# A cosine-attention and MLP-mixer kernel: token MLP per head pair, transposes by DMA, loads and norm work moved

## The chip, the cores and the metric

The kernel runs on one core of a Trainium2 chip. The metric is the device time of one execution in microseconds (us); lower is better. Every ratio is to runs of the kernel before on the same chip in the same rounds. A profiled span runs from the first to the last instruction of the core; a timed run is about 2 us longer than its own span. The profile of the kernel before is of an execution of 465.7 us, below the median of 467.4.

Engines in the profile: PE is TensorE (matmuls), PEld its weight loads, DVE is VectorE, ACT is ScalarE, POOL is GpSimd, SP is SyncE, which only issues DMAs. "L214" is a line of the kernel that was profiled.

## The reference

Eight batches, twelve heads, 448 tokens, head size 64. In float32:

```
q_n = q / (norm(q) + 1e-6);  k_n = k / (norm(k) + 1e-6)        # over the head dimension
attn = softmax(q_n @ k_n^T / tau)                              # tau = 0.1
x    = attn @ v                                                # to (8, 448, 768)
u    = x + (relu(x^T @ w_tok1) @ w_tok2)^T                     # token MLP, 448 -> 256 -> 448
out  = u + relu(u @ w_ch1) @ w_ch2                             # channel MLP, 768 -> 1536 -> 768
```

## The kernel before

The kernel works on 48 head pairs: 8 batches with 6 pairs each. One pass of its main loop, a *slot*, scores one pair and does the value matmuls of the pair before it. The mixer (both MLPs) waits in a queue, and a slot takes pieces from it to fill TensorE. The engines run in order, each through its own list of instructions, so the order in the text is the order on each engine.

The norms of a pair go through three engines: squares on POOL, the sum and the reciprocal on DVE, the root as a logarithm and an exponential on ACT. Then POOL scales.

```python
def squares(i, act_q=False):          # POOL (the first q on ACT)
    ...nc.gpsimd.tensor_mul(out=sq[:, a], in0=src, in1=src)
def sums(i):                          # DVE
    nc.vector.tensor_reduce(out=...["ssq"][...], in_=pipe[i]["sq"][:], axis=AXX.X, op=ALU.add)
def rnorms(n, p0=0, p1=HP):
    nc.scalar.activation(out=rn, in_=ssq, func=AF.Ln, bias=tiny[:])
    nc.scalar.activation(out=rn, in_=rn, func=AF.Exp, scale=0.5)
    nc.vector.tensor_scalar_add(out=rn, in0=rn, scalar1=EPS_NORM)      # 112 x 16 numbers, SBUF to SBUF
    nc.vector.reciprocal(out=rn, in_=rn)
def tpose(i):                         # 8 transposes on TensorE, one DVE copy
    ...
    for a, src in enumerate((st["kn"], st["qn"])):
        for c in range(NCH):
            nc.tensor.transpose(pst[:, a, c, :], src[:, c], id16[:SC, :SC])
    nc.vector.tensor_copy(out=qk[:], in_=pst[...])
```

The token MLP runs per batch, after the sixth pair. Its last step adds x to the product in PSUM with four identity matmuls that write runs of neighbouring columns:

```python
def m_tok1(b, tt, dh):                # 16 matmuls of 384 columns per batch
    ...
def m_tok2(b, dt):
    for tt in range(TT):
        nc.tensor.matmul(psU[:], rt16[b][:, tt, dt * 128:(dt + 1) * 128], w2t[...], ...)
    for m in range(4):
        nc.tensor.matmul(psU[:, lo:lo + (128 if m < 3 else 64)], x16[b][:, m, ...], rhs, ...)
    nc.vector.tensor_copy(out=ut[:, dt, span(b)], in_=psU[:])
```

## Time and profile before

| | before |
|---|---|
| median of timed runs | 467.4 us (466.4 to 468.4) |
| profiled span | 463.9 us |
| PE busy | 415.4 us (90%) |
| last matmul ends near | 459 us |

The page of the kernel before shows the span in 40 slices of 11.6 us. A digit is the busy share of a slice in tenths; PEclk is the clock granted to TensorE.

```profile
PE   0505889999999999999999999999999999999995
PEclk9999999999999999999999999999999999999998
```

TensorE is full from the seventh slice to the end, and starved before. The waits view of PE names what ended its idle time (columns: waiting instruction and its line, the instruction it waited for, us in total, times, longest). First, the stretch from 0 to 70 us:

```profile
PE psS_1_290 L199 <- ACT pt_251 L201: 11.0, 1, 11.0
PE pst_145 L183 <- DVE kn_143 L175: 9.1, 1, 9.1
PE psS_0_400 L199 <- DVE qk_365 L185: 3.8, 1, 3.8
```

From 70 us on, PE waited six times for an exponential, each time 1.1 us, and that is nearly all:

```profile
PE psS_0_1336 L199 <- ACT pt_1236 L201: 1.1, 1, 1.1
```

The timeline (start us, busy us, engine, line, what) shows the price of each kind of work in the full stretch. The distance between starts counts here, not the busy time, as matmuls overlap.

```profile
231.66 0.54 PE L246 MATMUL psU_4_3258<-w2t,rt_3_2919 128*128 128x448 f16 x2
232.04 0.36 PE L252 MATMUL psU_4_3258<-id_86,x_3_2062 128*128 128x128 f16 x4
232.24 0.36 PE L183 MATMUL pst_3266<-id_86,kn_3056 112*128 112x112 f16 x4
232.44 0.36 PE L183 MATMUL pst_3266<-id_86,qn_3054 112*128 112x112 f16 x4
```

Four transposes take 0.20 us (232.24 to 232.44), and the four identity matmuls of the token MLP take 0.20 us too (232.04 to 232.24).

### The profile page before, as it was taken

What the parts mean: (1) busy time and instruction counts of PE and PEld (TensorE: products, weight loads), DVE (VectorE), ACT (ScalarE), POOL (GpSimd) and SP (SyncE); (2) the same over time, 40 slices, a digit from 0 to 9 for tenths busy, and PEclk for the clock granted to TensorE, in tenths of its full rate; (3) what the DMA queues carried; (4) which work ended last, traced back from release to release, by engine and by line L of the source; (5) the groups of instructions that cost most, each with busy time, mean ns of one, the idle gap of its engine ahead of it and who ended that gap; (6) DMA issues with size and microseconds to landing.
All of it is one profiled execution on the core that took longest, in us unless ns stands there. A gap on an engine that the chain in (4) does not pass through costs nothing.

```text
span 463.9 us, 9519 instructions
## 1 busy us (share of the span) xinstructions
PE 415.4 (90%) x4136; PEld 250.1 (54%) x4136; DVE 218.9 (47%) x442; ACT 232.1 (50%) x262; POOL 218.8 (47%) x220
## 2 busy tenths in 40 slices
PE   0505889999999999999999999999999999999995
PEld 0203556556654566555655566556655666556563
DVE  2558659555564455445645445445735343224000
ACT  2324666775467544574457443674367534520410
POOL 4699698678374834374383725474472200000000
PEclk9999999999999999999999999999999999999998
DMA  9997999951485046721574065902100001000012
GB/s 205 237 235 175 223 204 229 209 120 32 125 188 119 1 129 154 167 47 37 134 192 102 1 165 117 206 9 78 52 35 1 35 35 56 15 34 35 34 54 83
DMA packets 72842, 50.02 MB, mean 108 GB/s; under 512 B 44449, under 2 KB 68449, under 8 KB 72801
## 3 DMA queue, kind: packets, MB, share of 16 engines
q1 hardware_dynamic: 69408, 44.05, 39.6%
q0 software_dynamic: 3392, 5.37, 6.3%
q8 instruction: 32, 0.52, 0.5%
q14 instruction: 10, 0.07, 0.1%
HBM read 43.78 MB, written 11.01 MB: 118 GB/s over the span
## 4 chain that ended last, share of the span: by engine, by line
PE 84%; ACT 6%; DVE 4%; POOL 2%; issue 2%; DMA 1%; SPq 0%; ACTq 0%; POOLq 0%
DMA qh_105<-in_q_dram 1%; DVE kn_324 L175 1%; DVE ssq_118 L157 1%; ACT pt_630 L201 1%; ACT pt_482 L201 1%; ACT pt_1042 L201 1%; DVE ssq_126 L157 0%; POOL sq_207 L152 0%; PE psF_2_1_5429 L279 0%; PE psF_2_0_5377 L279 0%; PE psF_1_1_5303 L279 0%; PE psF_0_0_5164 L279 0%; PE psF_2_1_4787 L279 0%; PE psF_2_0_4717 L279 0%; PE psF_1_1_4651 L279 0%
## 5 line engine op out<-in xcount | busy, mean ns | idle before, releaser
L260 PEld LDWEIGHTS <-wc1t 128*128 128x128 f16 x576 | 51.5, 97 | 52.0 <-issue 10.7
L279 PEld LDWEIGHTS <-gt_2_3862 128*128 128x128 f16 x168 | 15.3, 98 | 12.8 <-issue 2.6
L279 PEld LDWEIGHTS <-gt_1_2351 128*128 128x128 f16 x168 | 15.4, 98 | 12.5 <-issue 2.6
L279 PEld LDWEIGHTS <-gt_0_804 128*128 128x128 f16 x168 | 15.5, 98 | 11.4 <-issue 1.5
L279 PEld LDWEIGHTS <-gt_3_5342 128*128 128x128 f16 x168 | 15.9, 98 | 9.6
L228 PEld LDWEIGHTS <-w1t 128*128 128x128 f16 x128 | 10.9, 97 | 8.0 <-issue 2.6
L199 PE MATMUL psS_1_290<-qk_185 64*128 64x448 f16 x4 | 0.9, 557 | 11.0 <-ACT pt_251 L201 11.0
L183 PE MATMUL pst_145<-id_86,kn_143 112*128 112x112 f16 x4 | 0.6, 291 | 9.1 <-DVE kn_143 L175 9.1
L199 PEld LDWEIGHTS <-qk_185 64*128 64x128 f16 x8 | 0.5, 104 | 13.6 <-issue 12.9
L285 DVE COPY ost_0_6031<-psF_0_0_6032 128x384 f32<-128x384 f32 x1 | 0.6, 557 | 15.2 <-PE psF_0_0_6032 L282 15.2
L164 ACT ACTIVATE rn_119<-ssq_118,tiny 112x16 f32<-112x16 f32 x3 | 0.9, 307 | 12.1 <-DVE ssq_118 L157 12.1
L175 POOL TENSOR_TENSOR qn_5044<-qh_4311,rn_4315 112x512 f16<-112x512 f32 x1 | 1.0, 1041 | 10.3 <-DVE rn_4315 L167 10.3
L164 ACT ACTIVATE rn_109<-ssq_108,tiny 112x16 f32<-112x16 f32 x3 | 0.9, 304 | 8.6 <-DVE ssq_108 L157 8.6
L183 PEld LDWEIGHTS <-kn_143 112*128 112x128 f16 x4 | 0.3, 129 | 9.1 <-DVE kn_143 L175 9.1
L175 DVE TENSOR_TENSOR kn_324<-kh_116,rn_119 112x512 f16<-112x512 f32 x1 | 4.7, 4745 | 0.0
L282 PEld LDWEIGHTS <-ut_0_803 128*128 128x128 f16 x42 | 3.5, 98 | 1.8
L282 PEld LDWEIGHTS <-ut_1_2350 128*128 128x128 f16 x42 | 3.5, 98 | 1.8
L282 PEld LDWEIGHTS <-ut_2_3861 128*128 128x128 f16 x42 | 3.5, 98 | 1.8
L282 PEld LDWEIGHTS <-ut_3_5341 128*128 128x128 f16 x42 | 3.5, 98 | 1.8
L175 POOL TENSOR_TENSOR qn_3954<-qh_3191,rn_3195 112x512 f16<-112x512 f32 x1 | 1.0, 1042 | 7.3 <-PE psU_3_3986 L252 7.3
L199 PE MATMUL psS_0_400<-qk_365 64*128 64x448 f16 x4 | 0.9, 564 | 3.8 <-DVE qk_365 L185 3.8
L152 POOL TENSOR_TENSOR sq_2301<-qh_2033 112x512 f32<-112x512 f32 x1 | 1.0, 1039 | 6.9 <-DVE ssq_1701 L157 6.9
(1726 smaller groups left out, 1299.7 us busy)
## 6 DMA issues: line engine op xcount, KB each, us to landing
wc1t<-in_moe_w_ch_dram POOLq DMA_DIRECT2D x2, 1152.0 KB, 13.0
wc2t<-in_moe_w_ch_dram POOLq DMA_DIRECT2D x2, 1152.0 KB, 15.4
vs_107<-in_v_dram SPq DMA_DIRECT2D x1, 672.0 KB, 7.8
qh_115<-in_q_dram SPq DMA_DIRECT2D x1, 672.0 KB, 10.2
kh_116<-in_k_dram SPq DMA_DIRECT2D x1, 672.0 KB, 12.2
vs_117<-in_v_dram SPq DMA_DIRECT2D x1, 672.0 KB, 8.3
qh_123<-in_q_dram SPq DMA_DIRECT2D x1, 672.0 KB, 10.8
kh_124<-in_k_dram SPq DMA_DIRECT2D x1, 672.0 KB, 12.6
```

Source lines behind the costliest of these rows:

```text
L152: nc.gpsimd.tensor_mul(out=sq[:, a], in0=src, in1=src)
L157: nc.vector.tensor_reduce(out=half[i // HP]["ssq"][:, :, lo:lo + 2 * NCH], in_=pipe[i]["sq"][:], axis=AXX.X, op=ALU.add)
L164: nc.scalar.activation(out=rn, in_=ssq, func=AF.Ln, bias=tiny[:])
L175: eng.tensor_tensor(out=dst[:].rearrange("p c g e -> p g c e"), in0=src, in1=_bcast_free(rn, E), op=ALU.mult)
L183: nc.tensor.transpose(pst[:, a, c, :], src[:, c], id16[:SC, :SC])
L199: nc.tensor.matmul(psS[:, hh, j, 0:S], qk[hb:hb + 64, c * SC:c * SC + 128], qk[hb:hb + 64, S:2 * S], start=True, stop=True)
L201: nc.scalar.activation(out=st["pt"][:, cg], in_=psS[0:SC, :, :, 0:S], func=AF.Exp, scale=inv_tau)
L228: nc.tensor.matmul(psR[:], w1t[:, m, tt * 128:(tt + 1) * 128], x16[b][:, m, dh * DH:(dh + 1) * DH], start=(m == 0), stop=(m == 3))
L260: nc.tensor.matmul(psG[:], wc1t[:, dt, ct * 128:(ct + 1) * 128], ut[:, dt, span(b)], start=(dt == 0), stop=(dt == DT - 1))
L279: nc.tensor.matmul(psF[:], rows(gt, ct), wc2t[:, ct, dh * DH:(dh + 1) * DH], start=(ct == 0), stop=False)
L282: nc.tensor.matmul(psF[:, 128 * i:128 * (i + 1)], rows(ut, 3 * dh + i), id16[:], start=False, stop=(i == 2))
L285: nc.vector.tensor_copy(out=o[:, 0:DH], in_=psF[:])
```

## The change

It moves work off the full TensorE and fills its empty start. Four parts:

1. The token MLP runs per head pair, one slot behind the pair's value matmuls, instead of per batch.
2. q is loaded like k, in runs of 1 KB instead of 256 B. Token 4p+c then sits in partition p, chunk c, so the tokens of x are permuted as well. w_tok1 is loaded in that order; the identity matmuls put x back in order by writing every fourth column of PSUM.
3. From pair 12 on, q and k are transposed by DMA, issued from SyncE two slots ahead.
4. The norm work of early pairs starts later, three slots ahead, and each early pair has its own norms.

```diff
-    def tpose(i): ...for every pair
+    DMA_FROM = 12
+    def dma_tpose(i):
+        for a, src in enumerate((st["kn"], st["qn"])):
+            nc.sync.dma_start_transpose(out=qk[:, a], in_=src[:].rearrange("p c g e -> p (c g e)"))
 ...
-            nc.tensor.matmul(psR[:], w1t[:, m, tt * 128:(tt + 1) * 128],
-                             x16[b][:, m, dh * DH:(dh + 1) * DH], start=(m == 0), stop=(m == 3))
+    def m_tok1(i):
+        for tt in range(TT):
+            for m in range(NCH):
+                nc.tensor.matmul(psR[:, tt, :], w1t[:, m, tt * 128:(tt + 1) * 128], st["x"][:, m, :], ...)
 ...
-        for m in range(4):
-            nc.tensor.matmul(psU[:, lo:lo + (128 if m < 3 else 64)], x16[b][...], rhs, ...)
+        for c in range(NCH):
+            nc.tensor.matmul(psU[:].rearrange("d (p c) -> d c p", c=NCH)[:, c, :], st["x"][:, c, :],
+                             id16[:, LEAD[c]:LEAD[c] + SC], start=False, stop=(c == NCH - 1))
 ...
+    load_at = at({p: p - 6 if p < 13 else max(p - 8, (p - 1) // 2) for p in range(9, NP_ALL)})
+    sq_at = at({p: p - 3 if p < 10 else max(p - 6, 2 + p // 2) for p in range(3, NP_ALL)})
+    sc_at = at({p: p - 2 if p < DMA_FROM else p - 3 for p in range(2, NP_ALL)})
+    tok_at = at({p: max(p + 2, 3 if p < 1 else 4) for p in range(NP_ALL)})
 ...
+            for p in sc_at.get(i, ()):  scaled(p, dve="k" if p < 4 else "")
+            for p in sq_at.get(i, ()):  squares(p)
+            if i in (7, 8):             weights_ch2(i - 7)
+            if (i + 2) % HP == 0 ...:   cast_v((i + 2) // HP)
             (score, value matmuls, token MLP, pieces of the channel MLP)
+            for p in sq_at.get(i, ()):
+                sums(p)
+                if p < 15:              rnorm1(p)
```

More of the change, by code (lines that the diff above doesn't have):

```diff
@@ L49 @@
     NPAIR = H // 2
+    NP_ALL = B * NPAIR
     HP = 3
-    REM = S - 3 * 128
+    NHALF = 2 * B
     inv_tau = 1.0 / float(tau)
     EPS_NORM = 1e-6
-    COLS = (0, 128, 256, S - 128)
+    COLS = (0, SC, 2 * SC, S - 128)
+    LEAD = (0, 0, 0, 128 - SC)
+    DMA_FROM = 12
     cst = ctx.enter_context(tc.tile_pool(name="cst", bufs=1))
     qkv = ctx.enter_context(tc.tile_pool(name="qkv", bufs=3))
-    nrm = ctx.enter_context(tc.tile_pool(name="nrm", bufs=2))
+    nrm = ctx.enter_context(tc.tile_pool(name="nrm", bufs=3))
     att = ctx.enter_context(tc.tile_pool(name="att", bufs=3))
     ptp = ctx.enter_context(tc.tile_pool(name="ptp", bufs=2))
-    xp = ctx.enter_context(tc.tile_pool(name="xp", bufs=2))
     mix = ctx.enter_context(tc.tile_pool(name="mix", bufs=2))
@@ L78 @@
     nc.gpsimd.memset(tiny[:], 1e-18)
-    w1t = cst.tile([128, 4, T], FP16, name="w1t")
+    w1t = cst.tile([128, NCH, T], FP16, name="w1t")
     w2t = cst.tile([128, TT, S + 384], FP16, name="w2t")
@@ L83 @@
     wc2t = cst.tile([128, CT, D], FP16, name="wc2t")
+    nc.gpsimd.memset(w1t[:], 0.0)
     NV = 3
@@ L90, with weights_ch1, weights_ch2, load_qk @@
         vts.append(vt)
-    NHALF = 2 * B
     half = {}
     pipe = {}
-    x16 = {}
     pairt = {}
     def weights_tok():
-        nc.gpsimd.memset(w1t[0:64, 3, :], 0.0)
-        nc.gpsimd.dma_start(out=w1t[:, 0:3, :],
-                            in_=moe_w_tok1[0:384].rearrange("(c p) t -> p c t", p=128))
-        nc.gpsimd.dma_start(out=w1t[64:128, 3, :], in_=moe_w_tok1[384:448])
-        w2r = moe_w_tok2.rearrange("(tt p) s -> p tt s", p=128)
-        nc.gpsimd.dma_start(out=w2t[:, :, 0:S], in_=w2r)
-        nc.gpsimd.dma_start(out=w2t[:, :, S:S + 384], in_=w2r[:, :, 0:384])
-    def weights_ch1():
-        for i in range(2):
-            nc.gpsimd.dma_start(out=wc1t[:, 3 * i:3 * i + 3, :],
-                                in_=moe_w_ch1[384 * i:384 * (i + 1)].rearrange("(t p) c -> p t c", p=128))
-    def weights_ch2():
-        for i in range(2):
-            nc.gpsimd.dma_start(out=wc2t[:, 6 * i:6 * i + 6, :],
-                                in_=moe_w_ch2[768 * i:768 * (i + 1)].rearrange("(t p) d -> p t d", p=128))
-    def load_qk(n, lo=0, hi=6):
-        b, h0 = n // 2, 6 * (n % 2)
+        w1r = moe_w_tok1.rearrange("(p c) t -> p c t", c=NCH)
+        nc.gpsimd.dma_start(out=w1t[0:SC, 0:3, :], in_=w1r[:, 0:3, :])
+        nc.gpsimd.dma_start(out=w1t[128 - SC:128, 3, :], in_=w1r[:, 3, :])
+        nc.gpsimd.dma_start(out=w2t[:, :, 0:S], in_=moe_w_tok2.rearrange("(tt p) s -> p tt s", p=128))
+    def weights_ch1(i):
+        n = C // 2
+        nc.gpsimd.dma_start(out=wc1t[:, :, n * i:n * i + n],
+                            in_=moe_w_ch1[:, n * i:n * i + n].rearrange("(t p) c -> p t c", p=128))
+    def weights_ch2(i):
+        nc.gpsimd.dma_start(out=wc2t[:, 6 * i:6 * i + 6, :],
+                            in_=moe_w_ch2[768 * i:768 * (i + 1)].rearrange("(t p) d -> p t d", p=128))
+    def load_qk(i):
+        n, j = i // HP, 2 * (i % HP)
+        b, h = n // 2, 6 * (n % 2) + j
         if n not in half:
@@ L125, in load_qk @@
                            rn=nrm.tile([SC, 2, 6 * NCH], FP32, name=f"rn_{n}", tag="rn"))
-        nc.sync.dma_start(out=half[n]["q"][:, lo:hi].rearrange("p g c e -> p (g c) e"),
-                          in_=q[b, h0 + lo:h0 + hi].rearrange("g (c p) e -> p (g c) e", p=SC))
-        nc.sync.dma_start(out=half[n]["k"][:, lo:hi].rearrange("p g c e -> p g (c e)"),
-                          in_=k[b, h0 + lo:h0 + hi].rearrange("g (p c) e -> p g (c e)", c=NCH))
+        for nm, src in (("q", q), ("k", k)):
+            nc.sync.dma_start(out=half[n][nm][:, j:j + 2].rearrange("p g c e -> p g (c e)"),
+                              in_=src[b, h:h + 2].rearrange("g (p c) e -> p g (c e)", c=NCH))
     def load_v(n):
@@ L142, in sides, with squares @@
         return hf["q"][:, j:j + 2], hf["k"][:, j:j + 2]
-    def squares(i, act_q=False):
+    def squares(i, on_act=False):
         st = pipe[i] = {}
-        sq = nrm.tile([SC, 2, 2 * NCH, E], FP32, name=f"sq_{i}", tag="sq")
+        sq = nrm.tile([SC, 2, 2 * NCH, E], FP32, name=f"sq_{i}", tag="sq", bufs=2)
         for a, src in enumerate(sides(i)):
             src = src.rearrange("p g c e -> p (g c) e")
-            if act_q and a == 0:
+            if on_act:
                 nc.scalar.activation(out=sq[:, a], in_=src, func=AF.Square)
@@ L167, in rnorms, with rnorm1, scaled @@
         nc.vector.reciprocal(out=rn, in_=rn)
-    def scaled(i, dve_k=False):
+    def rnorm1(i):
+        rnorms(i // HP, i % HP, i % HP + 1)
+    def scaled(i, dve=""):
         lo = 2 * NCH * (i % HP)
@@ L172, in scaled @@
             dst = pipe[i][nm] = att.tile([SC, NCH, 2, E], FP16, name=f"{nm}_{i}", tag=nm)
-            eng = nc.vector if dve_k and a else nc.gpsimd
+            eng = nc.vector if nm[0] in dve else nc.gpsimd
             rn = half[i // HP]["rn"][:, a, lo:lo + 2 * NCH].rearrange("p (g c) -> p g c", g=2)
@@ L176, in scaled, with qk_tile @@
                               in1=_bcast_free(rn, E), op=ALU.mult)
+    def qk_tile(i):
+        pipe[i]["qk"] = att.tile([128, 2, NCH, SC], FP16, name=f"qk_{i}", tag="qk")
+        return pipe[i]["qk"]
     def tpose(i):
@@ L183, in tpose @@
                 nc.tensor.transpose(pst[:, a, c, :], src[:, c], id16[:SC, :SC])
-        qk = att.tile([128, 2, S], FP16, name=f"qk_{i}", tag="qk")
-        nc.vector.tensor_copy(out=qk[:], in_=pst[:].rearrange("p a c s -> p a (c s)"))
-        st["qk"] = qk
+        nc.vector.tensor_copy(out=qk_tile(i)[:], in_=pst[:])
+    def dma_tpose(i):
+        st = pipe[i]
+        qk = qk_tile(i)
+        for a, src in enumerate((st["kn"], st["qn"])):
+            nc.sync.dma_start_transpose(out=qk[:, a], in_=src[:].rearrange("p c g e -> p (c g e)"))
     def score(i, cg):
         st = pipe[i]
-        qk = st["qk"][:].rearrange("p a s -> p (a s)")
+        qk = st["qk"][:].rearrange("p a c s -> p (a c s)")
         if cg == 0:
@@ L204, in pv @@
         st = pipe[i]
-        b, pj = i // NPAIR, i % NPAIR
-        if b not in x16:
-            x16[b] = xp.tile([128, 4, D], FP16, name=f"x16_{b}", tag="x16")
+        if hh == 0:
+            st["x"] = att.tile([128, NCH, 128], FP16, name=f"x_{i}", tag="x")
         vt = half[i // HP]["vt"]
         g = 2 * (i % HP) + hh
-        hid = 2 * pj + hh
         psO = ps.tile([128, 4, E + 2], FP32, name=f"psO_{i}_{hh}", tag="b")
@@ L217, in pv @@
         nc.vector.reciprocal(out=rec[:], in_=psO[:, :, E])
-        nc.vector.tensor_tensor(out=x16[b][:, :, hid * E:(hid + 1) * E], in0=psO[:, :, 0:E],
+        nc.vector.tensor_tensor(out=st["x"][:, :, hh * E:(hh + 1) * E], in0=psO[:, :, 0:E],
                                 in1=_bcast_free(rec[:], E), op=ALU.mult)
-    rt16 = {}
-    def m_tok1(b, tt, dh):
-        if b not in rt16:
-            rt16[b] = mix.tile([128, TT, D], FP16, name=f"rt16_{b}", tag="rt16", bufs=1)
-        psR = ps.tile([128, DH], FP32, name=f"psR_{b}_{tt}_{dh}", tag="b")
-        for m in range(4):
-            nc.tensor.matmul(psR[:], w1t[:, m, tt * 128:(tt + 1) * 128],
-                             x16[b][:, m, dh * DH:(dh + 1) * DH], start=(m == 0), stop=(m == 3))
-        nc.vector.tensor_scalar_max(out=rt16[b][:, tt, dh * DH:(dh + 1) * DH], in0=psR[:], scalar1=0.0)
+    def m_tok1(i):
+        st = pipe[i]
+        psR = ps.tile([128, TT, 128], FP32, name=f"psR_{i}", tag="b")
+        for tt in range(TT):
+            for m in range(NCH):
+                nc.tensor.matmul(psR[:, tt, :], w1t[:, m, tt * 128:(tt + 1) * 128], st["x"][:, m, :],
+                                 start=(m == 0), stop=(m == NCH - 1))
+        st["r"] = att.tile([128, TT, 128], FP16, name=f"r_{i}", tag="r")
+        nc.vector.tensor_scalar_max(out=st["r"][:], in0=psR[:], scalar1=0.0)
     def span(b):
@@ L237, in place, with m_tok2 @@
         return 128 * m if b % 2 == 0 else (64 + 128 * m if m < 3 else 0)
-    def m_tok2(b, dt):
+    def m_tok2(i):
+        st = pipe[i]
+        b, dt = i // NPAIR, i % NPAIR
         if b // 2 not in pairt:
@@ L243, in m_tok2 @@
         ut = pairt[b // 2][0]
-        psU = ps.tile([128, S], FP32, name=f"psU_{b}_{dt}", tag="b")
+        psU = ps.tile([128, S], FP32, name=f"psU_{i}", tag="b")
         for tt in range(TT):
-            nc.tensor.matmul(psU[:], rt16[b][:, tt, dt * 128:(dt + 1) * 128],
-                             w2t[:, tt, 0:S] if b % 2 == 0 else w2t[:, tt, 384:384 + S],
+            nc.tensor.matmul(psU[:], st["r"][:, tt, :], w2t[:, tt, 0:S],
                              start=(tt == 0), stop=False)
-        for m in range(4):
-            lo = place(b, m)
-            rhs = id16[:] if m < 3 else id16[:, 64:128]
-            nc.tensor.matmul(psU[:, lo:lo + (128 if m < 3 else 64)], x16[b][:, m, dt * 128:(dt + 1) * 128], rhs,
-                             start=False, stop=(m == 3))
-        nc.vector.tensor_copy(out=ut[:, dt, span(b)], in_=psU[:])
+        for c in range(NCH):
+            nc.tensor.matmul(psU[:].rearrange("d (p c) -> d c p", c=NCH)[:, c, :], st["x"][:, c, :],
+                             id16[:, LEAD[c]:LEAD[c] + SC], start=False, stop=(c == NCH - 1))
+        if b % 2 == 0:
+            nc.vector.tensor_copy(out=ut[:, dt, 0:S], in_=psU[:])
+        else:
+            nc.vector.tensor_copy(out=ut[:, dt, S + 64:2 * S], in_=psU[:, 0:384])
+            nc.vector.tensor_copy(out=ut[:, dt, S:S + 64], in_=psU[:, 384:S])
     def m_ch1(b, ct):
@@ L295, in ns, with ch_units @@
         return n * cols / 2.4
-    def mixer_units(b):
-        first = [(ns(DH, 4), lambda tt=tt, dh=dh: m_tok1(b, tt, dh)) for dh in range(NDH) for tt in range(TT)]
-        first += [(ns(3 * S), lambda dt=dt: m_tok2(b, dt)) for dt in range(DT)]
-        return first, [(ns(S, DT), lambda ct=ct: m_ch1(b, ct)) for ct in range(CT)]
-    def out_units(b):
-        return [(ns(DH, 13), lambda m=m, dh=dh: m_ch2(b, m, dh))
-                for m in range(3 + b % 2) for dh in range(NDH)]
-    def braid(a, c):
-        got, i, j = [], 0, 0
-        while i < len(a) or j < len(c):
-            if j >= len(c) or (i < len(a) and i * len(c) <= j * len(a)):
-                got.append(a[i]); i += 1
-            else:
-                got.append(c[j]); j += 1
-        return got
-    NP_ALL = B * NPAIR
+    def ch_units(b):
+        return ([(ns(S, DT), lambda ct=ct: m_ch1(b, ct)) for ct in range(CT)]
+                + [(ns(DH, 13), lambda m=m, dh=dh: m_ch2(b, m, dh))
+                   for m in range(3 + b % 2) for dh in range(NDH)])
     queue = []
-    fed = [0.0, 0.0]
+    fed = [0.0]
     def feed(budget, least=0.0):
@@ L328, in feed, with at @@
             done += t
-        fed[1] += done
+    def at(slots):
+        got = {}
+        for p, s in slots.items():
+            got.setdefault(s, []).append(p)
+        return got
+    load_at = at({p: p - 6 if p < 13 else max(p - 8, (p - 1) // 2) for p in range(9, NP_ALL)})
+    sq_at = at({p: p - 3 if p < 10 else max(p - 6, 2 + p // 2) for p in range(3, NP_ALL)})
+    sc_at = at({p: p - 2 if p < DMA_FROM else p - 3 for p in range(2, NP_ALL)})
+    tok_at = at({p: max(p + 2, 3 if p < 1 else 4) for p in range(NP_ALL)})
@@ L331 @@
     with tc.manual_schedule():
-        load_qk(0, 0, 2)
-        load_qk(0, 2, 6)
+        load_qk(0)
+        load_qk(1)
         load_v(0)
-        load_qk(1)
+        for p in range(2, 5):
+            load_qk(p)
         load_v(1)
-        load_qk(2)
-        squares(0, act_q=True)
+        for p in range(5, 9):
+            load_qk(p)
+        squares(0, on_act=True)
         sums(0)
-        rnorms(0, 0, 1)
-        squares(1)
-        scaled(0, dve_k=True)
+        rnorm1(0)
+        squares(1, on_act=True)
@@ L343 @@
+        squares(2)
+        scaled(0, dve="qk")
         tpose(0)
-        squares(2)
+        cast_v(0)
         sums(1)
-        rnorms(0, 1, 2)
-        cast_v(0)
-        score(0, 0)
-        scaled(1, dve_k=True)
-        tpose(1)
-        score(0, 1)
-        sums(2)
-        rnorms(0, 2, 3)
-        scaled(2, dve_k=True)
-        weights_tok()
-        squares(3)
-        sums(3)
-        rnorms(1, 0, 1)
-        for i in range(NP_ALL + 1):
-            b, pj = i // NPAIR, i % NPAIR
-            if i + 8 >= 9 and (i + 8) % HP == 0 and (i + 8) // HP < NHALF:
-                load_qk((i + 8) // HP)
-            if i % HP == 0 and i // HP + 2 < NHALF:
-                load_v(i // HP + 2)
-            if i == 0:
-                squares(4)
-                scaled(3, dve_k=True)
-            if i == 1:
-                squares(5)
-                scaled(4, dve_k=True)
-                cast_v(1)
-                weights_ch1()
-            if i == 2:
-                scaled(5, dve_k=True)
-            if i >= 4 and i + 2 < NP_ALL:
-                scaled(i + 2)
-            if 6 <= i + 6 < NP_ALL:
-                squares(i + 6)
-            if i == 6:
-                weights_ch2()
-            if (i + 3) % HP == 0 and 2 <= (i + 3) // HP < NHALF:
-                cast_v((i + 3) // HP)
-            quota = sum(t for t, _ in queue) / (NPAIR - pj + 1) if queue else 0.0
-            if i == NP_ALL:
-                pv(i - 1, 0)
-                pv(i - 1, 1)
-            else:
-                if i:
-                    score(i, 0)
-                feed(quota * 0.3)
-                if i:
-                    pv(i - 1, 0)
-                feed(quota * 0.2, 500.0)
-                if i and i + 1 < NP_ALL:
-                    tpose(i + 1)
-                if i:
-                    score(i, 1)
-                feed(quota * 0.3)
-                if i:
-                    pv(i - 1, 1)
-                feed(quota * 0.2)
-            if i < 2:
-                sums(4 + i)
-                rnorms(1, 1 + i, 2 + i)
-            if i >= 1 and i + 5 < NP_ALL:
-                sums(i + 5)
-                if (i + 5) % HP == 2:
-                    rnorms((i + 5) // HP)
-            if pj == 0 and i:
-                first, second = mixer_units(b - 1)
-                queue += braid(first, out_units(b - 2) if b >= 2 else []) + second
@@ L412 @@
-        queue += out_units(B - 1)
+        rnorm1(1)
+        scaled(1, dve="qk")
+        sums(2)
+        rnorm1(2)
+        for i in range(NP_ALL + 2):
+            for p in load_at.get(i, ()):
+                load_qk(p)
+            if (i + 4) % HP == 0 and 2 <= (i + 4) // HP < NHALF:
+                load_v((i + 4) // HP)
+            if DMA_FROM <= i + 2 < NP_ALL:
+                dma_tpose(i + 2)
+            for p in sc_at.get(i, ()):
+                scaled(p, dve="k" if p < 4 else "")
+            for p in sq_at.get(i, ()):
+                squares(p)
+            if i == 0:
+                weights_tok()
+            if i in (2, 4):
+                weights_ch1(i // 4)
+            if i in (7, 8):
+                weights_ch2(i - 7)
+            if (i + 2) % HP == 0 and 1 <= (i + 2) // HP < NHALF:
+                cast_v((i + 2) // HP)
+            left = 6 - (i - 2) % NPAIR
+            quota = max(sum(t for t, _ in queue) - 2000.0, 0.0) / left
+            if i < NP_ALL:
+                score(i, 0)
+            feed(quota * 0.25)
+            if 0 < i <= NP_ALL:
+                pv(i - 1, 0)
+            for p in tok_at.get(i, ()):
+                m_tok1(p)
+            feed(quota * 0.25, 400.0)
+            if i + 1 < min(DMA_FROM, NP_ALL):
+                tpose(i + 1)
+            if i < NP_ALL:
+                score(i, 1)
+            for p in tok_at.get(i, ()):
+                m_tok2(p)
+                if p % NPAIR == NPAIR - 1:
+                    queue += ch_units(p // NPAIR)
+            feed(quota * 0.25)
+            if 0 < i <= NP_ALL:
+                pv(i - 1, 1)
+            feed(quota * 0.25)
+            for p in sq_at.get(i, ()):
+                sums(p)
+                if p < 15:
+                    rnorm1(p)
+                elif p % HP == HP - 1:
+                    rnorms(p // HP)
```

## The prediction

> **What bounds the kernel now.** Two stages. From about 68 us on TensorE is saturated: the table of 12 us windows shows PE busy 12.00 of 12 in most, the waits view after 70 us only six waits of 1.1 us (exp, L201). Until 68 us it starves: the timeline shows seven pairs scored and no mixer work, the waits view stalls of 11.0, 9.1, 3.8 us. Scores there cost 0.93 us against 0.55 later. The last matmul ends near 459 us, the span at 464; timed runs are 3.6 us above it.
>
> **Work of TensorE**, from starts of consecutive instructions in the timeline, once warm: transposes 49 ns (8 per pair: 0.39 us), scores 1.15 us per pair, value matmuls 1.04, token MLP per batch 2.6 + 3.5, channel MLP 13.7 + 14.8. Sum 401 us. Check: 382 left at 68 us (7.5 pairs done); 68 + 382 + 7 of waits = 457 against 459 seen.
>
> **Removed, added, moved.**
> - Transposes of pairs 12 to 47: 36 x 0.39 = 14 us off the critical engine, and 36 DVE copies of 0.62 us, not critical. Instead 72 DMA transposes of 112 KB. The Trainium skill ("DMA: Bandwidth & Descriptors", section "Latency and other measured facts") gives 261 GB/s for a transpose with a non-contiguous middle dimension; I estimate from it 0.44 us of transfer each; no run here shows one yet. Issued two slots (16 us) early, they should hide.
> - Token MLP per pair: 48 matmuls of 128 columns at about 56 ns for 16 of 384 at 163 ns: equal. It fills 5 us of the idle start. I assume that the strided PSUM write of the identity matmuls is free.
> - q in 1 KB runs: packets in the first 25 us took 0.066 ns/B against 0.094 for 256 B. But the first exp now queues behind the norms of pair 2, which wait for its load: near 15 us.
> - Early norms: each early slot has a chain sums 1.2, ln and exp 0.6, add and reciprocal 0.5, two POOL scalings 2.1, two POOL squares 2.1, sums: 6.5 us (first two slots 6), above the 5.4 us that score, exp and the single score buffer cost. Slots 0 to 6 end near 59 us, slot 7 near 67; channel units start in slot 8.
>
> **Sum.** From about 69 us TensorE is saturated, with 8.5 pairs, 6.5 token units and two channel units done (30 us of work). 387 - 30 = 357 left; 69 + 357 + 4 of waits + 5 for the last output = 435 us of span; plus 3.6: **438 us**, 8 in 10 between 427 and 451. Chances: faster 0.94, within 2% 0.05, slower 0.01.
>
> **What would show each step.** Groups: 96 transposes on PE instead of 384. PE waits after 70 us: under 5 us in sum, none on a transposed qk tile. Timeline: exps of consecutive pairs 6 to 7 us apart in slots 2 to 6; first channel matmul at 63 to 70 us; token matmuls 56 ns apart, strided identity ones 49 ns. Packets of 256 B gone.
>
> **What would make it wrong.** DMA transposes of several us each, or held behind output stores on SyncE, so that scores wait: tens of us slower. Strided PSUM writes at half rate: +9 us. A start paced by 5.4 us instead of 6.5: 8 us faster. POOL and DVE slowing each other (one DVE scaling took 4.7 us): a few us slower.

## The result, and the profile after

| | before | after |
|---|---|---|
| median of timed runs | 467.4 us | 456.6 us (455.9 to 456.8) |
| ratio to before | 1 | 0.977 (0.974 to 0.979) |
| profiled span | 463.9 us | 455.0 us |
| PE busy | 415.4 us | 408.4 us |

Ratios in this text are the mean time of one kernel's fast runs over that of the other's in the same rounds, with a 95% interval, so they are not quite ratios of the medians quoted beside them. The change made the kernel 2.3% faster, where the prediction said 6.3%. The miss is 18.6 us.

The slices of the kernel after (11.4 us each) differ from those before in two places. TensorE starts earlier, but it is not full until the ninth slice, and the granted clock drops twice, which the windows below tell apart.

```profile
PE   1377572899999999999999999999999999999995
PEclk9999987899999999999999999999999999999998
```

The windows view gives, for a stretch of 12 us, the busy time of PE, PEld, DVE, ACT and POOL, then the granted clock (0.86 and 0.57 here), the DMA share and GB/s:

```profile
48.00:60.00 12.00, 7.25 (x90) 4.97 (x88) 6.57 (x18) 7.48 (x8) 9.00 (x9) 0.86 0.75 133
72.00:84.00 12.00, 5.44 (x25) 2.77 (x26) 7.99 (x8) 3.41 (x4) 8.48 (x9) 0.57 0.96 160
```

The waits view of PE after 70 us has a wait that was not there before:

```profile
PE pst_990 L188 <- DVE x_950 L225: 8.1, 1, 8.1
PE psS_1_1136 L208 <- ACT pt_1078 L210: 1.9, 1, 1.9
```

A transpose waits 8.1 us for a PSUM buffer that DVE has to empty (the write of x_950). What held DVE stands in its timeline:

```profile
69.20 0.17 DVE L164 TENSOR_SCALAR rn_382<-rn_382 112x16 f32<-112x16 f32 x1 [0.62 <-ACT rn_382 L163]
69.58 1.16 DVE L155 TENSOR_REDUCE ssq_381<-sq_822 112x16 f32<-112x1024 f32 x1
71.36 6.27 DVE L164 TENSOR_SCALAR rn_382<-rn_382 112x16 f32<-112x16 f32 x1 [0.62 <-ACT rn_382 L163]
77.66 0.25 DVE L165 RECIPROCAL rn_382<-rn_382 112x16 f32<-112x16 f32 x1
77.99 0.42 DVE L225 TENSOR_TENSOR x_950<-psO_0_951,rec_0_968 128x256 f16<-128x256 f32 x1
```

The same add of 1e-6 to 112x16 numbers takes 0.17 us for one pair and 6.27 us for the next. POOL's timeline next to it shows a cast, six instructions without a gap, and then the issue of a load:

```profile
70.14 1.48 POOL L135 CAST vt_95<-vs_380 112x1536 f16<-112x1536 f32 x1
71.57 1.05 POOL L176 TENSOR_TENSOR qn_924<-qh_378,rn_382 112x512 f16<-112x512 f32 x1
...
76.57 1.03 POOL L150 TENSOR_TENSOR sq_931<-kh_702 112x512 f32<-112x512 f32 x1
77.55 0.88 POOL L112 DMA_DIRECT2D wc2t<-in_moe_w_ch_dram  x1
```

The long add ends at 77.63 us (71.36 plus 6.27), when POOL's run of six ends. On PE the stall is followed by a slow stretch:

```profile
69.15 1.30 PE L269 MATMUL psG_1_982<-ut_0_448,wc1t 128*128 128x448 f16 x6
78.56 0.53 PE L188 MATMUL pst_990<-id_83,kn_817 112*128 112x112 f16 x4 [8.11 <-DVE x_950 L225]
81.64 2.49 PE L269 MATMUL psG_2_1016<-ut_0_448,wc1t 128*128 128x448 f16 x6
```

The same six matmuls took 1.30 us before the stall and 2.49 us after it. The clock in the window of 72 to 84 us was 0.57.

The second loss is small in each place and everywhere. The token MLP of one pair, in the full stretch:

```profile
238.08 0.55 PE L254 MATMUL psU_3436<-w2t,r_3420 128*128 128x448 f16 x2
238.47 0.55 PE L257 MATMUL psU_3436<-id_83,x_3248 128*128 128x112 f16 x4
238.81 1.34 PE L269 MATMUL psG_5_3444<-ut_1_1783,wc1t 128*128 128x448 f16 x6
```

The four identity matmuls now occupy 0.34 us (238.47 to 238.81), against 0.20 us before, although each has fewer columns (112 against 128). After the first matmul of such a group the next start follows in 54 ns, after each of the others in 96 (medians).

The rest went about as planned. PE makes 96 transposes instead of 384, and the waits view of PE shows none for a tile that a DMA transposed.

### The profile page after: what moved, and what is told of

Read it like the earlier page. It is cut to its first block, busy times and chain, and to the rows that moved or that the text cites. A ratio compares the mean times of both kernels' runs of the same rounds, so it can differ in the third digit from the quotient of the medians.

```text
span 455.0 us, 9700 instructions
## 1 busy us (share of the span) xinstructions
PE 408.4 (90%) x4104; PEld 250.4 (55%) x4104; DVE 202.8 (45%) x458; ACT 236.8 (52%) x277; POOL 213.5 (47%) x216
## 4 chain that ended last, share of the span: by engine, by line
PE 80%; DVE 7%; ACT 6%; POOL 4%; issue 2%; DMA 1%; SPq 0%; ACTq 0%; POOLq 0%
DVE rn_382 L164 1%; DVE ssq_130 L155 1%; DVE ssq_381 L155 1%; DMA kh_104<-in_k_dram 1%; ACT pt_308 L210 1%; DVE ssq_118 L155 1%; DVE ssq_704 L155 0%; PE psG_2_1016 L269 0%; PE psF_1_0_3760 L288 0%; PE psF_1_0_2231 L288 0%; PE psF_0_0_2105 L288 0%; PE psF_2_1_1719 L288 0%; PE psF_1_0_5275 L288 0%; PE psF_1_1_1595 L288 0%; PE psF_0_1_1466 L288 0%
## 5 line engine op out<-in xcount | busy, mean ns | idle before, releaser
L269 PEld LDWEIGHTS <-wc1t 128*128 128x128 f16 x576 | 53.8, 101 | 45.1 <-issue 7.2
L233 PEld LDWEIGHTS <-w1t 128*128 128x128 f16 x384 | 22.7, 98 | 0.0
L288 PEld LDWEIGHTS <-gt_0_449 128*128 128x128 f16 x168 | 15.7, 98 | 10.9 <-issue 1.9
L288 PEld LDWEIGHTS <-gt_3_4834 128*128 128x128 f16 x168 | 15.9, 98 | 9.3
L288 PEld LDWEIGHTS <-gt_1_1784 128*128 128x128 f16 x168 | 15.8, 98 | 9.4 <-issue 0.4
L288 PEld LDWEIGHTS <-gt_2_3305 128*128 128x128 f16 x168 | 15.7, 98 | 9.5 <-issue 0.4
L164 DVE TENSOR_SCALAR rn_382<-rn_382 112x16 f32<-112x16 f32 x3 | 6.6, 2206 | 1.9 <-ACT rn_382 L163 1.9
L176 POOL TENSOR_TENSOR qn_5263<-qh_4628,rn_4632 112x512 f16<-112x512 f32 x1 | 1.0, 1043 | 13.5 <-DVE rn_4632 L165 13.5
L176 POOL TENSOR_TENSOR qn_3745<-qh_3099,rn_3103 112x512 f16<-112x512 f32 x1 | 1.0, 1042 | 13.5 <-DVE rn_3103 L165 13.5
L176 POOL TENSOR_TENSOR qn_2216<-qh_1570,rn_1574 112x512 f16<-112x512 f32 x1 | 1.0, 1043 | 12.4 <-DVE rn_1574 L165 12.4
L176 POOL TENSOR_TENSOR qn_4510<-qh_3880,rn_3884 112x512 f16<-112x512 f32 x1 | 1.0, 1042 | 12.4 <-DVE rec_0_4542 L224 12.4
L176 POOL TENSOR_TENSOR qn_2981<-qh_2351,rn_2355 112x512 f16<-112x512 f32 x1 | 1.0, 1042 | 11.3 <-DVE rec_0_3013 L224 11.3
L176 POOL TENSOR_TENSOR qn_2611<-qh_1952,rn_1956 112x512 f16<-112x512 f32 x1 | 1.0, 1042 | 11.1 <-DVE rn_1956 L165 11.1
L176 POOL TENSOR_TENSOR qn_1839<-qh_1193,rn_1197 112x512 f16<-112x512 f32 x1 | 1.0, 1042 | 10.5 <-DVE rn_1197 L165 10.5
L176 POOL TENSOR_TENSOR qn_1452<-qh_808,rn_812 112x512 f16<-112x512 f32 x1 | 1.0, 1042 | 10.1 <-PE psO_0_1485 L221 10.1
L176 POOL TENSOR_TENSOR qn_4132<-qh_3481,rn_3485 112x512 f16<-112x512 f32 x1 | 1.0, 1044 | 9.6 <-DVE rn_3485 L165 9.6
L176 POOL TENSOR_TENSOR qn_4889<-qh_4246,rn_4250 112x512 f16<-112x512 f32 x1 | 1.0, 1042 | 9.0 <-DVE rn_4250 L165 9.0
## 6 DMA issues: line engine op xcount, KB each, us to landing
vs_117<-in_v_dram SPq DMA_DIRECT2D x1, 672.0 KB, 10.7
```

Source lines behind the costliest of these rows:

```text
L176: eng.tensor_tensor(out=dst[:].rearrange("p c g e -> p g c e"), in0=src, in1=_bcast_free(rn, E), op=ALU.mult)
L233: nc.tensor.matmul(psR[:, tt, :], w1t[:, m, tt * 128:(tt + 1) * 128], st["x"][:, m, :], start=(m == 0), stop=(m == NCH - 1))
L269: nc.tensor.matmul(psG[:], wc1t[:, dt, ct * 128:(ct + 1) * 128], ut[:, dt, span(b)], start=(dt == 0), stop=(dt == DT - 1))
L288: nc.tensor.matmul(psF[:], rows(gt, ct), wc2t[:, ct, dh * DH:(dh + 1) * DH], start=(ct == 0), stop=False)
```

## The experiments

Ten kernels were run, each timed in three rounds against the kernel before. All gave the right result except the first. The gains quoted below are differences of medians against the change. Worked out from the two ratios instead, they agree within 1.2 us, except for e1_contig: 4.9 us, not 6.8.

| run | what | median us | ratio to before |
|---|---|---|---|
| (the change) | | 456.6 | 0.977 |
| e1_contig | identity matmuls write neighbouring columns | 449.8 | 0.966 |
| e2_norm | norms without the VectorE add and reciprocal | 443.1 | 0.950 |
| e10_noadd | norms without the VectorE add only | 447.7 | 0.958 |
| e3_wch2 | weight load in other slots | 451.4 | 0.968 |
| e5_dose | four POOL instructions in the run, not six | 452.4 | 0.969 |
| e8_swap | cast before the weight load | 459.1 | 0.982 |
| e4_nodma | no DMA transposes | 470.3 | 1.008 |
| e6_order | e2, and a correct form of e1 | 434.9 | 0.931 |
| e7_start | e6 with another order of norm work | 442.4 | 0.947 |
| e9_start2 | e6 with a third order | 430.2 | 0.921 |

### The stride in PSUM

```diff
-            nc.tensor.matmul(psU[:].rearrange("d (p c) -> d c p", c=NCH)[:, c, :], st["x"][:, c, :], ...
+            nc.tensor.matmul(psU[:, c * SC:(c + 1) * SC], st["x"][:, c, :], ...
```

> The four identity matmuls that add x into psU write 112 neighbouring columns instead of every fourth column; nothing else changes. The result is wrong on purpose (x is added to the wrong tokens). Theory: the stride in PSUM doubles each of these 192 matmuls from 49 to 95 ns, 8.8 us in all, of which the part after saturation is lost: starts 49 ns apart and the time 7 to 9 us below the changed kernel (near 449 us). Rival (95 ns comes from the weight loads of x, which are as many and as large as before): still 95 ns, and no change of the time.

Measured: 449.8 us, 6.8 us below the change. The runs lie in two groups near 448 and 452 us. In the timeline of this run the same group of four costs 0.20 us (234.38 to 234.58) again, with the same weight loads:

```profile
234.38 0.36 PE L257 MATMUL psU<-id,x 128*128 128x112 f16 x4
234.58 1.30 PE L269 MATMUL psG<-ut,wc1t 128*128 128x448 f16 x6
```

So the stride of the write is the cost: 0.14 us per pair (0.34 minus 0.20), 6.7 us over 48 pairs, which lies between the two readings of the time (6.8 by medians, 4.9 by ratios). The Trainium skill, page "SBUF — State Buffer", section "Door 1: The DMA port swizzle", says that PSUM has lines of 8 bytes (two fp32) and that a non-contiguous PSUM access pattern slows matmuls significantly. The trace agrees: with a step of 16 bytes, starts lie 96 ns apart instead of 49. I had not looked this up before predicting.

### What held the VectorE add

```diff
# e2_norm
-        nc.scalar.activation(out=rn, in_=rn, func=AF.Exp, scale=0.5)
-        nc.vector.tensor_scalar_add(out=rn, in0=rn, scalar1=EPS_NORM)
-        nc.vector.reciprocal(out=rn, in_=rn)
+        nc.scalar.activation(out=rn, in_=rn, func=AF.Exp, scale=-0.5)
```

> The reciprocal norm is made by one more Exp on ScalarE (scale -0.5 instead of 0.5), and the VectorE add of 1e-6 and the reciprocal go. Theory: the 8.1 us stall of TensorE at 70 to 78 us was one VectorE add of 112x16 that took 6.3 us[...]. Without that instruction the stall and the half clock after it go (8 to 11 us), and each early slot's chain is 0.5 us shorter (up to 4 us over eight slots): 10 to 14 us faster, near 444 us. Rival (the stall is the chain of two pairs of squares in slot 7, whatever VectorE does): the exp of pair 8 still waits, most of the stall stays, at most 4 us faster.

Measured: 443.1 us, 13.5 us below the change. The wait of 8.1 us is down to 0.3 us:

```profile
PE pst L186 <- DVE x L223: 0.3, 1, 0.3
```

The first channel matmul starts at 63.2 us instead of 67.0; this share of the gain is the shorter chain, not the stall; e10 below sets it apart.

```diff
# e3_wch2
-            if i in (7, 8):
-                weights_ch2(i - 7)
+            if i in (5, 6):
+                weights_ch2(i - 5)
```

> The two loads of the second channel weight move from slots 7 and 8 to slots 5 and 6; nothing else changes. In both kernels the long VectorE instruction began just after GpSimd had issued a weight load of 1.1 MB. Rival: writing that load's descriptors is what held VectorE; then no VectorE instruction over 2 us near 70 us, and 8 to 11 us faster. Theory: what held it is the run of six GpSimd instructions without a gap (two scalings, four squares); they still follow each other, so that the add still takes 4 to 6 us and the time is within 2 us.

Measured: 451.4 us (449.2 to 453.8), and neither theory was met. The longest add now took 1.52 us and the stall of PE 2.7 us. The trace says why the test was not clean. Without the 0.88 us issue in front, POOL's cast came earlier and met the add of the *other* pair, on which POOL's next scaling depends. So POOL stopped after the cast and there was no run:

```profile
69.90 1.45 POOL L135 CAST vt<-vs 112x1536 f16<-112x1536 f32 x1
71.82 1.04 POOL L176 TENSOR_TENSOR qn<-qh,rn 112x512 f16<-112x512 f32 x1 [0.47 <-DVE rn L165]
```

```profile
69.87 1.52 DVE L164 TENSOR_SCALAR rn<-rn 112x16 f32<-112x16 f32 x1 [0.62 <-ACT rn L163]
```

The add waited until the cast ended (71.35), which the theory says, but the run does not rule out the load. Two sharper tests followed.

```diff
# e5_dose: pair 13's squares go from slot 8 to slot 9, pair 15's from 9 to 10
+    sq_at = at({p: p - 3 if p < 10 else {13: 9, 15: 10}.get(p, max(p - 6, 2 + p // 2)) for p in range(3, NP_ALL)})
```

> One pair of squares (pair 13) moves from slot 8 to slot 9 (and pair 15 from 9 to 10), so that GpSimd runs four instructions without a gap after the cast of v in slot 7, not six; all else as in the changed kernel. Theory: the VectorE add that arrives during that cast is held until GpSimd's run ends, so it takes about 4.3 us instead of 6.3, the stall of TensorE falls from 8.1 to about 6 us, and the time by 2 us or so. Rival (the hold has a length of its own, or comes from the weight load's descriptors, issued at the same time as before): 6.3 us again.

Measured: two POOL instructions fewer, 2.00 us less hold. The add took 4.27 us and ended at 74.95, with POOL's run of four:

```profile
70.68 4.27 DVE L164 TENSOR_SCALAR rn<-rn 112x16 f32<-112x16 f32 x1 [0.62 <-ACT rn L163]
```

```profile
73.89 1.03 POOL L150 TENSOR_TENSOR sq<-kh 112x512 f32<-112x512 f32 x1
74.87 0.88 POOL L112 DMA_DIRECT2D wc2t<-in_moe_w_ch_dram  x1
```

The longest wait of PE for DVE fell to 6.1 us. The time, 452.4 us, fell by 4 us, more than the 2 expected.

```diff
# e8_swap: in slot 7 the cast of v first, then the weight load
-            if i in (7, 8):  weights_ch2(i - 7)
             if (i + 2) % HP == 0 ...:  cast_v((i + 2) // HP)
+            if i in (7, 8):  weights_ch2(i - 7)
```

> In slot 7 GpSimd makes the cast of v before it issues the load of the second channel weight, not after; the same work in the other order. Theory: the late VectorE add, at about 71.4 us, then meets the issue of a DMA, next to which other adds took 0.17 us; it is not held, the stall goes, 8 to 11 us faster. Rival (descriptors being written hold VectorE): the add is held as long or longer, and nothing is gained.

Measured: my expectation failed. The add met the last 0.2 us of the load's issue and was held for 6.27 us all the same, until the six instructions were done at 78.8 us:

```profile
71.84 0.88 POOL L112 DMA_DIRECT2D wc2t<-in_moe_w_ch_dram  x1
72.75 1.06 POOL L176 TENSOR_TENSOR qn<-qh,rn 112x512 f16<-112x512 f32 x1
```

```profile
72.54 6.27 DVE L164 TENSOR_SCALAR rn<-rn 112x16 f32<-112x16 f32 x1 [0.62 <-ACT rn L163]
```

So it does not matter whether the add meets the cast or the load's issue. The length of the hold follows the run of POOL instructions behind it: 6.27 us for six, 4.27 for four (with the same load in front), 1.52 where POOL paused after the cast. A hold of a fixed length, set by the load, is ruled out by that. The median of 459.1 us is 2.5 us above the change. The profile places this surplus in the start (the first exponential of slot 10 comes at 99.1 us, in the change at 96.2), but its cause stays open.

```diff
# e10_noadd
-        nc.vector.tensor_scalar_add(out=rn, in0=rn, scalar1=EPS_NORM)
```

> Of the norms only the VectorE add of 1e-6 goes (the error is 1e-6 of the norm); the VectorE reciprocal stays, in place and from SBUF to SBUF. Theory: it is the add that cannot run beside GpSimd's run; the reciprocal, at the same point of time, is not held. The 8.1 us stall goes and the slots get shorter by only 0.2 us each: 10 to 12 us faster than the changed kernel, 445 to 447 us. Rival (any VectorE instruction between SBUF and SBUF is held there): the reciprocal takes about 6 us instead, and the time stays within 3 us.

Measured: 447.7 us, 8.8 us below the change. The first channel matmul comes no earlier (67.3 us), but slot 8 takes 9.0 us between first exponentials, in the change 17.9: this gain is the stall. The reciprocal stands where the add stood, in place, SBUF to SBUF, next to the same run of POOL, and is not held:

```profile
71.31 0.25 DVE L164 RECIPROCAL rn<-rn 112x16 f32<-112x16 f32 x1 [0.62 <-ACT rn L163]
```

```profile
70.62 1.05 POOL L175 TENSOR_TENSOR qn<-qh,rn 112x512 f16<-112x512 f32 x1
71.62 1.04 POOL L175 TENSOR_TENSOR kn<-kh,rn 112x512 f16<-112x512 f32 x1
```

The add arrived 0.21 us before POOL's next instruction, this reciprocal 0.31 us before. Three more reciprocals that arrived 0.10 to 0.17 us before one, within a POOL run, were not held either, as this one at 80.33 us:

```profile
80.33 0.25 DVE L164 RECIPROCAL rn<-rn 112x16 f32<-112x16 f32 x1 [0.62 <-ACT rn L163]
```

So the hold depends on which VectorE instruction stands there, not only on DVE's place in the chain. The Trainium skill, page "SBUF — State Buffer", section "Who interferes with whom", says that VectorE's tensor_scalar can use a pair of SBUF ports that it shares with GpSimd, and that the later one is blocked for the whole instruction of the other. The runs agree in kind, though none of them shows the port itself. They differ in length: the wait was not one GpSimd instruction (1.0 us) but a whole run of six.

One thing stays open: a run without a gap does not suffice. Other adds that arrived in the middle of a POOL run (in the kernel after at 89.24 us, 0.44 us before the next instruction) took 0.52 us, thus got in at the next boundary. The adds that were held for a whole run all arrived 0.21 us before its first instruction: in the change, e5 and e8, and in e1 (6.27 us) and e4 (6.26 us), which kept the run of six. Closer arrivals go both ways: 0.09 us before an instruction in e4 the add took 0.17 us, 0.03 us before the cast in e3 it took 1.52. No run set that distance on purpose, so whether the moment of arrival decides is not shown.

### The DMA transposes

```diff
-    DMA_FROM = 12
+    DMA_FROM = 48
```

> DMA transposes undone: pairs 12 to 47 are transposed on TensorE again (and scaled two slots ahead, not three). Theory: 36 pairs at 0.39 us come back to the saturated TensorE, 14 us slower, near 470 us, all of it after 105 us. Rival (the DMA transposes gave little, because scores wait for them or because the SyncE queue holds loads back): within 5 us of the changed kernel.

Measured: 470.3 us, 13.7 us above the change and 0.8% above the kernel before. The stall (8.1 us) and the stride are still in this run, so the difference is the transposes (with the scaling two slots ahead again, not three). They are worth what was expected of them; without them the rest of the change, with its two losses, gains nothing.

### A version that beats both

e6_order keeps the tokens permuted to the very end. The identity matmuls write neighbouring columns, w_tok2 gets its columns reordered once on GpSimd, and the output rows are stored in pieces with a step of four rows.

```diff
+            if i == 2:
+                nc.gpsimd.tensor_copy(out=w2t[:].rearrange("q t (c p) -> q t c p", c=NCH),
+                                      in_=w2s[:].rearrange("q t (p c) -> q t c p", c=NCH))
 ...
+                    nc.sync.dma_start(out=out[bb].rearrange("(p c) d -> p c d", c=NCH)[j % SC:j % SC + n, j // SC, :],
+                                      in_=o[r:r + n])
```

> Correct version of the contiguous PSUM write, on top of the norms without VectorE: the tokens stay in the permuted order through both MLPs; the second token weight is loaded plainly and reordered once on GpSimd (about 1 us), and each output tile is stored in pieces of rows of one residue. Theory: both losses are independent, so their gains add: 443.1 minus 6.8 = 436 us, correct. Rival (smaller stores or the reordering cost something of it): 438 to 443.

Measured: 434.9 us, correct. The two gains add.

```diff
# e7_start: squares before scalings on POOL; score(0, 0) before sums(2); in each slot:
             tpose(i + 1)
+            for p in sq_at.get(i, ()):  sums(p); rnorm1(p)
             score(i, 1)
```

> As the version with contiguous PSUM writes and norms without VectorE, and besides: GpSimd squares pair i+3 before it scales pair i+2, the sums and norms stand before the second score of a slot, and the first score before the norms of pair 2. Theory: the early slots were paced by the chain sums, norm, two scalings, two squares, sums (6.0 us or more); without it by score, exp and the one score buffer (5.4 us): eight slots at 0.7 to 1 us and up to 4 us from the first exp: 6 to 11 us faster than the version before it. Rival (the early pace is set by something else, as loads or GpSimd's total work): within 3 us.

Measured: 442.4 us, 7.5 us *slower* than e6. The chain that I wanted to cut was cut, but a new one appeared, as engines run in order. The sums now stood on DVE behind the copy of the next pair's transposes, those on PE behind the first score, and the second exponential on ACT behind the norms. In slots 1 to 3 the second exponential started 3.9 to 4.3 us after the first; in e6 it was 2.3 to 2.5 us.

```diff
# e9_start2: as e7, but in slots 1 to 6 the norms stand right behind the first score
             score(i, 0)
+            if 0 < i < 7:  norms()
```

> A second try at the start. In the first one the sums stood behind the copy of the next pair's transposes on VectorE, so the second exp of each slot waited 4 us. Now, in slots 1 to 6 the sums and norms stand right behind the first score, before the value matmuls' evictions; from slot 7 on they stand at the end as in the version with contiguous PSUM writes and norms without VectorE. Theory: early slots take 5.2 to 5.9 us instead of 5.9 to 6.6 and the first exp comes 4 us earlier: channel work starts 4 to 9 us earlier, time 427 to 432 us. Rival (GpSimd's total work paces the early slots): within 2 us of 434.9.

Measured: 430.2 us (428.5 to 431.8), 0.921 of before. The first channel matmul starts at 57.1 us, in e6 at 62.2. Slots 2 to 6 took 4.6 to 5.4 us, in e6 5.9 to 6.5 (distances of their first exponentials). Slots 0 and 1 gave part of it back, with nearly 8 us each. The slices (10.7 us each) show a TensorE that is nearly full from the fourth slice, and a clock that never drops:

```profile
PE   1469889999999999999999999999999999999995
PEclk9999999999999999999999999999999999999999
```

## Why the prediction was wrong

The direction was right, and so were the two gains it counted on: fewer transposes and an earlier start on a TensorE that bounds. Two other steps of the sum failed, and the start came later than said. Point by point:

- **Transposes off TensorE, 14 us.** Right: undoing them cost 13.7 us. They hide, as said: the 72 DMA transposes landed 2.4 to 7.4 us after their issue (median 3.1), and were issued two slots ahead. The page "DMA: Bandwidth & Descriptors" gave 261 GB/s, and the estimate from it was 0.44 us each. In the trace the packets of one transpose take 0.73 us (median), which is 157 GB/s, so the estimate was too low. That cost nothing: issuing one took SyncE about 1.26 us (median), and its packets moved after that.
- **Token matmuls of 128 columns, 56 ns.** Right: eight took 0.45 us in the kernel after.
- **Early slots of 6 to 6.5 us.** Nearly right: first exponentials lie 6.0 to 6.7 us apart in slots 0 to 5, and 7.4 in slot 6. The first channel matmul came at 67.0 us, inside the predicted 63 to 70. But the first exponential came at 16.9 us instead of 15, and slot 7 ended at 71.2 us, when 67 was said.
- **"I assume that the strided PSUM write of the identity matmuls is free."** This step failed. It was named as a risk (+9 us), but not put into the sum. Without the stride the change ran 6.8 us faster.
- **"From about 69 us TensorE is saturated", with "4 of waits".** This step failed. Mixer work had begun before 69 us (the first channel matmul at 67.0), but PE then stalled for 8.1 us behind one held VectorE add and ran at half clock until about 84 us. The kernel before had the sign of it, a VectorE scaling of 4.7 us next to POOL (it began 0.16 us before a run of five POOL instructions and ended during the fifth), and the prediction put it at "a few us". Without the add the change ran 8.8 us faster.
- **Packets of 256 B gone.** Only from the loads: the first 25 us have none, but the DMA transposes move in packets of 256 B.

The two failed steps sum to 15.6 us (6.8 and 8.8; 13.8 by the ratios), and 456.6 minus 15.6 is 441.0 us, inside the range. The remaining 3 to 5 us fit the later start (slot 7 ended 4 us late), which no run isolates. The version with both losses repaired, e6_order, took 434.9 us, but part of that is a gain that the prediction did not count: without the reciprocal too, the early chain is shorter (e2 is 4.6 us below e10).

## What to carry to other kernels

An instruction of 0.2 us can cost 9 us when it is held behind a neighbour engine's run of work without a gap; before giving a neighbour bursts, look for such instructions in the chain and make them elsewhere (here one sign in an exponential did it). A layout change that pushes a permutation into the writes of matmuls should be priced per matmul, or the permutation carried on to a place where it is free, as the rows of an output store. Moving an instruction forward on one in-order engine moves it behind something else there: follow the new order on every engine before expecting the gain.

## What the Trainium skill lacked or had wrong

- "SBUF — State Buffer", who interferes with whom: it says that the blocked engine waits for the other's instruction. Here the blocked VectorE add waited for a whole run, 6.27 us for six GpSimd instructions and 4.27 us for four, yet in other places 0.52 us, one boundary. The page has no rule for this.
- The same page's note on PSUM lines gives no figure, nor does the page "PSUM — Partial Sum Buffer", which has the note too: here matmuls with 112 columns and a step of four fp32 started 96 ns apart, and 49 ns apart without the step.
- "TensorE: Matmul & The Clock Gate", section "Why this matters for your kernels", warns of idle gaps above about 3 us. Here the clock fell to 0.58 (56 to 60 us) around a wait of 2.3 us that ended at 56.9 us, the last of several: the score behind it took 0.93 us instead of 0.55. Whether this wait alone did it is not shown.
- "DMA: Bandwidth & Descriptors" has no time in us for issuing a DMA transpose on trn2 (only cycles of earlier generations), and no figure for one small transpose: here 1.26 us of SyncE for 112 KB from SBUF to SBUF, 0.73 us of packets (157 GB/s, against the page's 261 on another kernel), and 2.4 to 7.4 us from issue to landing.
